# Truer times, a port rule and split output tasks in the list scheduler of a linear-attention and token-mixing kernel

## The chip, the cores and the metric

The kernel runs on one core of a Trainium2 chip. The metric is the time of one execution on the device, in microseconds (us), lower is better. A run counts as slow when it is over 1.5% above the fastest of its kernel.

Engines are named as in the profile: PE does matmuls, DVE is the vector engine, ACT the scalar engine, POOL the GpSimd engine, and SP issues the loads and stores. An instruction line of a profile reads: start, duration, engine, source line, operation, output <- inputs, shape, and in square brackets how long the engine sat idle before it and what ended that wait.

## The reference, cut to what matters

```python
# batch 4, 8 heads, 768 tokens, head size 48
for t in range(S):                       # linear attention with decay
    y[t]  = r[t] @ (state + (u * k[t]) v[t]^T)
    state = w * state + k[t] v[t]^T
x = y as (4, 768, 384)
theta = x @ w_theta
zr, zi = x * cos(theta), x * sin(theta)
y = w_tok_r @ zr + w_tok_i @ zi          # mixing over the 768 tokens
u = x + y
out = u + relu(u @ w_ch)
```

The kernel does the recurrence in chunks of 128 tokens. For a pair of chunks it scales r and k by powers of w (`Rw`, `Kw`), transposes both ("flips"), takes scores, masks them (`mAT`), updates the state (`outer`, `Y`, `Z`, `Sb`), adds the diagonal term (`PD`, `diag`, `dg`, `yd`) and gets `x`. Then come theta, `zr` and `zi`. When a batch is through, its `mix` and `chan` matmuls can run while the next batch is in its first part.

## The kernel before

The program is not written in the order in which it runs. Each piece is a task with an engine, an estimated time and a priority. A list scheduler goes through a simulated time and puts the tasks of each engine in an order; that order is then emitted and is fixed. The engines follow it strictly, each waiting at every task for its inputs (in the trace of before, shown below, PE stands idle for 1.94 us at one such task). So a wrong estimate doesn't change what is computed, only the order.

```python
    def order(self):
        ...
            for e in waiting:
                while free_at[e] <= now:
                    nfree = sum(1 for b in banks if b[0] <= now)
                    best = None
                    for t in waiting[e]:
                        if t.ready <= now and (not t.acq or len(t.acq) + t.keep <= nfree):
                            if best is None or (t.prio, t.seq) < (best.prio, best.seq):
                                best = t
                    ...
                    ns = t.ns
                    if e == PE:
                        if t.mode != last_mode:
                            ns += 100.0
                        last_mode = t.mode
                    free_at[e] = now + ns
...
    def dve_ns(n, rate=1.0):
        return n / (0.96 * rate) + 75
    def pool_ns(n):
        return 190 + 1.95 * n
...
            P.add(PE, 345, scores, rd=[kT, rT], acq=tk, prio=pb + 2, mode=1)
...
            def products(PD=PD, KT=KT, RT=RT):
                nc.vector.tensor_mul(PD, RT, KT)            # both inputs in SBUF
            P.add(DVE, dve_ns(2 * HP * C, 2.0), products, rd=[kT, rT], wr=[kP], prio=pb + 4)
...
            def outputs(...):        # the carried half (RT by Sb), then the inner half (mAT by vb)
            P.add(PE, 720, outputs, rd=[rT] + mk + [kv_] + [("Sb", ...)], acq=ty, prio=pb + 6, mode=1)
```

Of the kernel before, what the change touches and what calls it, by code (L numbers as in the profile page):

```python
# [29 lines left out]

KEEP = 0
LATENCY = {PE: 200.0, DVE: 150.0, ACT: 175.0, POOL: 160.0, SP: 2200.0}


class Task:
    __slots__ = ("eng", "ns", "fn", "deps", "prio", "seq", "lat", "acq", "uses", "nwait",
                 "users", "ready", "end", "mode", "keep")


class Plan:  # L40
# [8 lines left out]

    def add(self, eng, ns, fn, rd=(), wr=(), prio=0.0, lat=None, acq=(), use=(), mode=0, keep=0):  # L50
        t = Task()
        t.eng, t.ns, t.fn, t.prio, t.mode = eng, ns, fn, prio, mode
        t.keep = keep
        t.lat = LATENCY[eng] if lat is None else lat
        t.seq = len(self.tasks)
        t.acq, t.uses = list(acq), list(acq) + list(use)
        rd, wr = list(rd) + list(use), list(wr) + list(acq)
        deps = set()
        for k in rd:
            if k in self.writer:  # L60
                deps.add(self.writer[k])
        for k in wr:
            if k in self.writer:
                deps.add(self.writer[k])
            deps.update(self.readers.get(k, ()))
        for k in rd:
            self.readers.setdefault(k, set()).add(t)
        for k in wr:
            self.writer[k] = t
            self.readers[k] = set()  # L70
        for b in t.uses:
            self.bank_uses[b] = self.bank_uses.get(b, 0) + 1
        deps.discard(t)
        t.deps = deps
        self.tasks.append(t)
        return t

    def order(self):
# [6 lines left out]
        for t in self.tasks:  # L85
            if t.nwait == 0:
                waiting[t.eng].append(t)
        free_at = {e: 0.0 for e in waiting}
        last_mode = None
        banks = [(0.0, i) for i in range(self.nbanks)]  # L90
# [3 lines left out]
        while len(out) < n:  # L94
            for e in waiting:
                while free_at[e] <= now:
                    nfree = sum(1 for b in banks if b[0] <= now)
                    best = None
                    for t in waiting[e]:
                        if t.ready <= now and (  # L100
                                not t.acq or len(t.acq) + t.keep <= nfree):
                            if best is None or (t.prio, t.seq) < (best.prio, best.seq):
                                best = t
                    if best is None:
                        break
                    t = best
                    waiting[e].remove(t)
                    banks.sort()
                    for b in t.acq:
                        self.bank_of[b] = banks.pop(0)[1]  # L110
                    ns = t.ns
                    if e == PE:
                        if t.mode != last_mode:
                            ns += 100.0
                        last_mode = t.mode
                    free_at[e] = now + ns
                    done = now + ns
                    t.end = done + t.lat
                    out.append(t)
                    for b in t.uses:  # L120
                        left[b] -= 1
                        freed[b] = max(freed.get(b, 0.0), t.end)
                        if left[b] == 0:
                            banks.append((freed[b], self.bank_of[b]))
                    for x in t.users:
                        x.ready = max(x.ready, done if x.eng == e else t.end)
                        x.nwait -= 1
                        if x.nwait == 0:
                            waiting[x.eng].append(x)
# [19 lines left out]
def kernel(  # L149
# [91 lines left out]
    def setup():  # L241
# [24 lines left out]
        def pads(ts):  # L266
            for t in ts:
                nc.gpsimd.memset(t[:, :, :, D:], 0.0)
        P.add(POOL, 900, lambda: make_identity(nc, ident_f), wr=["ident_f"], prio=-98)
        P.add(DVE, 200, lambda: nc.vector.tensor_copy(ident, ident_f), rd=["ident_f"],  # L270
              wr=["ident"], prio=-98)
        P.add(POOL, 600, lambda: pads(Rws), wr=[(("Rw", i), j) for i in range(2) for j in range(2)], prio=-97)
# [78 lines left out]
    def token_weights(prio):  # L351
        for to in range(NCH):
            for src, dst, key in ((moe_w_tok_r, WrT, "WrT"), (moe_w_tok_i, WiT, "WiT")):
                i = load_rows(src[to * C:(to + 1) * C, :].rearrange("p (o c) -> p o c", o=2), 2)
                for sg in range(2):
                    tok = ("W", key, to, sg)

                    def flip(i=i, sg=sg, tok=tok):
                        for j in range(3):
# [3 lines left out]
                                             start=(j == 0), stop=(j == 2))  # L363
                    P.add(PE, 330, flip, rd=L2(i) + ["ident_f"], acq=[tok], prio=prio + to)

# [10 lines left out]
    def flip6(dst, blocks, tok, prio, rd, wr):  # L376
# [3 lines left out]
        def go():  # L380
            for i, s in enumerate(blocks):
                nc.tensor.matmul(bank16(tok)[:, i * C:(i + 1) * C], s, ident,  # L382
                                 is_transpose=True, start=(i == 0), stop=(i == n - 1))
        P.add(PE, 55 * n, go, rd=rd + ["ident"], acq=[tok], prio=prio, mode=0)
        P.add(ACT, act_ns(n * C), lambda: nc.scalar.activation(  # L385
# [4 lines left out]
    def front(b, base):  # L390
# [3 lines left out]
        for pr in range(NP):  # L394
# [5 lines left out]
            for c in range(2):  # L400
# [5 lines left out]
                          Ls[ir][:, c * HD:(c + 1) * HD].rearrange("p (h d) -> p h d", h=H), wpow),  # L406
                      rd=[("L", ir, c), "wpow"], wr=[(kR, c)], prio=pb)
            flip6(RT.rearrange("p a h t -> p (a h) t"),
# [6 lines left out]
            for c in range(2):  # L415
                P.add(DVE, dve_ns(HD), lambda c=c, Kw=Kw, ik=ik: nc.vector.tensor_mul(  # L416
                    Kw[:, c, :, :D],
                    Ls[ik][:, c * HD:(c + 1) * HD].rearrange("p (h d) -> p h d", h=H), wpinv),
                    rd=[("L", ik, c), "wpinv"], wr=[kK], prio=pb)
            flip6(KT.rearrange("p a h t -> p (a h) t"),  # L420
# [7 lines left out]
            for c in range(2):  # L428
# [5 lines left out]
                def scores(c=c, tk=tk, KT=KT, RT=RT):  # L434
                    for hp in range(HP):
                        for hi in range(2):
# [3 lines left out]
                                             start=(hp == 0), stop=(hp == HP - 1))  # L440
                P.add(PE, 345, scores, rd=[kT, rT], acq=tk, prio=pb + 2, mode=1)
                for hi in range(2):
# [5 lines left out]
            def products(PD=PD, KT=KT, RT=RT):  # L448
                nc.vector.tensor_mul(PD, RT, KT)  # L449
            P.add(DVE, dve_ns(2 * HP * C, 2.0), products, rd=[kT, rT], wr=[kP],  # L450
                  prio=pb + 4)
            td = ("dg", b, pr)

            def diag(td=td, PD=PD):
# [6 lines left out]
            P.add(PE, 200, diag, rd=[kP, "uw"], acq=[td], prio=pb + 4, mode=0)  # L461
            P.add(ACT, 70, lambda td=td, dg=dg: nc.scalar.activation(
                dg, bank(td)[:, :2 * H], Act.Copy), use=[td], wr=[kd], prio=pb + 4)
# [7 lines left out]
            def outer(ts=ts, Kw=Kw, vb=vb, cs=cs):  # L471
                for c in cs:
                    for hp in range(HP):
                        for hi in range(2):
# [5 lines left out]
                                stop=(c == cs[-1] and hp == HP - 1), skip_group_check=True)  # L480
            P.add(PE, 200 * len(cs), outer, rd=[kK, kv_], acq=[ts], prio=pb + 2, mode=2)
            for c in cs:
# [20 lines left out]

            def outputs(ty=ty, pr=pr, vb=vb, RT=RT):
                first = [True, True]
                for c in range(2):
                    cc = 2 * pr + c
                    if cc == 0:
                        continue
                    for hp in range(HP):  # L510
                        for hi in range(2):
                            q = slice(hi * Dp, (hi + 1) * Dp)
                            o = (c * HP + hp) * D
                            nc.tensor.matmul(bank(ty[hi])[:, o:o + D],
                                             RT[q, c, hp, :],
                                             Sb[q, cc - 1, hp, :], start=first[hi], stop=False,
                                             skip_group_check=True)
                            first[hi] = False
                for c in range(2):
                    mAT = mATs[(b * NCH + 2 * pr + c) % 6]  # L520
                    for hi in range(2):
                        for hp in range(HP):
                            o = (c * HP + hp) * D
                            nc.tensor.matmul(bank(ty[hi])[:, o:o + D], mAT[:, hi, hp, :],
                                             vb[:, c, 2 * hp + hi, :], start=first[hi],
                                             stop=(c == 1 and hp == HP - 1),
                                             skip_group_check=True)
                            first[hi] = False
            P.add(PE, 720, outputs, rd=[rT] + mk + [kv_] + [
                ("Sb", b % 2, 2 * pr + c - 1) for c in range(2) if 2 * pr + c > 0],  # L530
                acq=ty, prio=pb + 6, mode=1)
            for hi in range(2):
# [11 lines left out]
            for t in range(2):  # L544
# [3 lines left out]
                def theta(th=th, t=t, xT=xT):  # L548
                    for dk in range(ND):
                        nc.tensor.matmul(bank(th)[:, :HD], xT[:, t, dk, :], Wth[:, dk, :],  # L550
                                         start=(dk == 0), stop=(dk == ND - 1))
                P.add(PE, 495, theta, rd=[("xT", g % 2), ("Wth", 0), ("Wth", 2)], acq=[th],
                      prio=pb + 8, mode=0)
# [14 lines left out]
    def mixing(b, base):  # L568
        x, zr, zi = xs[b % 3], zrs[b % 2], zis[b % 2]
        xi, zj = b % 3, b % 2  # L570
        for to in range(NCH):
# [5 lines left out]
            for part in range(NP):  # L577
                def mix(tm=tm, to=to, part=part):
                    for j in range(2):
                        so = 2 * part + j  # L580
                        for i, (WT, z) in enumerate(((WrT, zr), (WiT, zi))):
                            nc.tensor.matmul(bank(tm)[:, :HD], WT[:, so, to * C:(to + 1) * C],  # L582
                                             z[:, so], start=(so == 0 and i == 0),
                                             stop=(so == NCH - 1 and i == 1))
                P.add(PE, 660, mix,
                      rd=[(n, zj, 2 * part + j) for n in ("zr", "zi") for j in range(2)]
# [9 lines left out]
            def chan(tf=tf, uT=uT):  # L596
                for dk in range(ND):
                    nc.tensor.matmul(bank(tf)[:, :HD], uT[:, dk, :], Wch[:, dk, :],
                                     start=(dk == 0), stop=(dk == ND - 1))
            P.add(PE, 495, chan, rd=[("uT", g % 3), ("Wch", 0), ("Wch", 2)], acq=[tf],  # L600
                  prio=pb + 1)
# [51 lines left out]
```

## Time and profile before

| | before |
|---|---|
| time, median of 4 runs | 158.73 us (158.64 to 159.06) |
| span of the profiled run | 157.8 us |
| PE, DVE, ACT, POOL busy | 135.7, 120.9, 93.0, 79.0 us |
| matmuls priced at their pace in the trace | 113.6 us |
| changes of PE mode (full-array matmuls and two kinds of half-array ones) | 72, about 95 ns each, 6.8 us |
| PE lost in 0-20, 20-120, 120 us to the last matmul | 15.2, 17.5, 1.8 us |

Busy time of PE is modelled, so each matmul is priced at the usual distance to the next start when PE has work and a full clock (162 ns for 384 columns, 56 ns for a bf16 flip, 109 ns for a float32 flip, 25 to 29 ns for small ones); mode changes are priced at 95 ns (after a mixing matmul the next start comes at 258 ns instead of 162); what a stretch of time holds beyond that is lost, to waits and to a lower clock.

From the page of the kernel before, the busy times:

```profile
PE 135.7 (86%) x1641; PEld 92.8 (59%) x1641; DVE 120.9 (77%) x221; ACT 93.0 (59%) x175; POOL 79.0 (50%) x94
```

From the same page, the span in 40 slices (about 3.9 us each); a digit is the busy share in tenths, and in the third line the granted clock of PE:

```profile
PE   0347789999999979988958999899999999999971
...
DVE  5449796896657999999998899977999956434441
...
PEclk9999999999999999999995699999999999999999
```

The windows view of before (time, then busy us and instructions of PE, PEld, DVE, ACT and POOL, the clock, the DMA share, GB/s), by stretch:

```profile
60.00:80.00 20.00, 18.64 (x287) 12.65 (x285) 20.00 (x37) 15.96 (x29) 15.37 (x18) 1.00 0.92 193
80.00:100.00 20.00, 17.56 (x223) 11.74 (x224) 18.77 (x31) 12.11 (x26) 15.95 (x15) 0.83 0.82 167
```

Over the whole trace of before, the 7 `Kw` and 2 `PD` with less than 30 ns of a POOL operation beside them take 542 to 560 and 678 to 681 ns; the other 17 and 10 take 541 to 1823 and 682 to 1475. The masks (`mAT`), with one input in PSUM, take 673 to 692 ns, beside POOL or not. PE, in the same moments (timeline of before):

```profile
81.80 0.35 PE L457 MATMUL bank_66<-uw,PD_113 128*128 128x2 bf16 x8 [1.94 <-DVE PD_113 L449]
...
82.46 1.03 PE L382 MATMUL bank_66<-ident,Rw_95 128*128 128x128 bf16 x8
...
84.14 1.01 PE L382 MATMUL bank_61<-ident,Kw_97 128*128 128x128 bf16 x8 [0.65 <-DVE mAT_116 L443]
```

PE's next task in the fixed order was the diagonal one, which needs `PD_113`, so PE stood still for 1.94 us. From 82.4 us its clock was half, for 6.8 us: the eight flips that take 0.61 us elsewhere take 1.0 here.

### The profile page before, as it was taken

The page shows a single profiled execution, that of the slowest core. Times are in us where ns is not written, and L with a number is a line of the kernel's source. Part 1 is how long each engine was busy: PE and PEld are TensorE (multiplying, and loading weights), DVE is VectorE, ACT ScalarE, POOL GpSimd, SP SyncE. Part 2 cuts the span into 40 slices and gives each one's busy share as a digit, 9 for nine tenths or more (in the row PEclk, how much of TensorE's full clock was granted, in tenths as well). Part 3 has the DMA queues.
Part 4 walks back from the last instruction along what each step waited for, and adds up shares of the span by engine and source line. Part 5 has one row for each costly group of instructions (what it writes and reads, how often), then busy time and mean ns, then how long its engine had stood idle before and what let it go on. Part 6 is the DMA issues. An engine that isn't in the chain of part 4 may idle for free.

```text
span 157.8 us, 4220 instructions
## 1 busy us (share of the span) xinstructions
PE 135.7 (86%) x1641; PEld 92.8 (59%) x1641; DVE 120.9 (77%) x221; ACT 93.0 (59%) x175; POOL 79.0 (50%) x94
## 2 busy tenths in 40 slices
PE   0347789999999979988958999899999999999971
PEld 0236565698776656656745667367767665666640
DVE  5449796896657999999998899977999956434441
ACT  3593576886955569785846576938935475212120
POOL 6228653650682479595798478526617544000000
PEclk9999999999999999999995699999999999999999
DMA  3999999899993999797989947593100021121212
GB/s 83 216 220 213 225 226 348 325 407 294 198 205 113 192 228 208 174 198 163 227 160 200 208 97 158 119 208 121 54 0 4 25 75 54 50 100 50 104 50 100
DMA packets 81083, 25.24 MB, mean 160 GB/s; under 512 B 75560, under 2 KB 79528, under 8 KB 81064
## 3 DMA queue, kind: packets, MB, share of 16 engines
q1 hardware_dynamic: 81040, 24.98, 65.1%
q8 instruction: 13, 0.21, 0.5%
q14 instruction: 6, 0.05, 0.1%
q10 hardware_dynamic: 24, 0.00, 0.0%
HBM read 20.25 MB, written 4.72 MB: 158 GB/s over the span
## 4 chain that ended last, share of the span: by engine, by line
PE 56%; DVE 22%; ACT 7%; issue 6%; DMA 5%; SPq 1%; POOL 0%; ACTq 0%; DVEq 0%; POOLq 0%
PE bank_64 L582 7%; PE bank_66 L582 5%; PE bank_62 L582 5%; PE bank_65 L582 4%; DMA ld_90<-in_v_dram 3%; DMA ld_86<-in_r_dram 3%; DVE Kw_98 L416 3%; DVE PD_113 L449 2%; DVE mAT_115 L443 2%; PE bank_63 L582 2%; DVE zr_136 L560 2%; PE bank_67 L382 2%; DVE mAT_116 L443 2%; PE bank_61 L382 2%; DVE Kw_97 L416 1%
## 5 line engine op out<-in xcount | busy, mean ns | idle before, releaser
L582 PEld LDWEIGHTS <-WrT 128*128 128x128 bf16 x144 | 14.3, 99 | 7.6 <-issue 0.3
L582 PEld LDWEIGHTS <-WiT 128*128 128x128 bf16 x144 | 14.3, 99 | 7.3 <-issue 0.3
L494 POOL TENSOR_TENSOR Z_122<-Y_120,wC 128x192 f32<-128x192 f32 x12 | 6.1, 507 | 12.8 <-DVE Y_120 L491 6.5
L563 POOL TENSOR_TENSOR zi_137<-x_132,sin_139 128x384 bf16<-128x384 bf16 x4 | 3.7, 943 | 9.9 <-ACT sin_139 L554 9.9
L494 POOL TENSOR_TENSOR Z_123<-Y_121,wC 128x192 f32<-128x192 f32 x8 | 5.3, 663 | 5.3 <-DVE Y_121 L491 5.3
L404 POOL TENSOR_TENSOR Rw_96<-ld_85,wpow 128x384 bf16<-128x384 f32 x6 | 6.2, 1048 | 3.5 <-PE bank_68 L382 3.5
L582 PE MATMUL bank_64<-zr_135,WrT 128*128 128x384 bf16 x18 | 5.9, 327 | 0.0
L582 PE MATMUL bank_64<-zi_137,WiT 128*128 128x384 bf16 x18 | 5.9, 326 | 0.0
L582 PE MATMUL bank_62<-zr_136,WrT 128*128 128x384 bf16 x18 | 5.9, 326 | 0.0
L582 PE MATMUL bank_62<-zi_138,WiT 128*128 128x384 bf16 x18 | 5.9, 326 | 0.0
L582 PE MATMUL bank_64<-zr_136,WrT 128*128 128x384 bf16 x18 | 5.9, 326 | 0.0
L582 PE MATMUL bank_64<-zi_138,WiT 128*128 128x384 bf16 x18 | 5.9, 326 | 0.0
L582 PE MATMUL bank_66<-zi_137,WiT 128*128 128x384 bf16 x18 | 5.9, 326 | 0.0
L582 PE MATMUL bank_66<-zr_135,WrT 128*128 128x384 bf16 x18 | 5.8, 325 | 0.0
L550 PEld LDWEIGHTS <-xT_141 128*128 128x128 bf16 x36 | 3.7, 107 | 3.3 <-issue 1.4
L404 POOL TENSOR_TENSOR Rw_95<-ld_88,wpow 128x384 bf16<-128x384 f32 x4 | 5.0, 1276 | 0.6 <-PE bank_67 L382 0.6
L449 DVE TENSOR_TENSOR PD_112<-RT_106,KT_110 128x1024 bf16<-128x1024 bf16 x3 | 3.3, 1092 | 2.6 <-ACT KT_110 L385 2.6
L404 POOL TENSOR_TENSOR Rw_96<-ld_91,wpow 128x384 bf16<-128x384 f32 x4 | 3.9, 997 | 2.2 <-DMA ld_91<-in_r_dram 2.2
L283 PE MATMUL bank_61<-ident_f,wu 8*128 8x8 f32 x1 | 0.2, 240 | 5.6 <-DMA wu<-in_u_dram 5.6
L563 POOL TENSOR_TENSOR zi_138<-x_132,sin_140 128x384 bf16<-128x384 bf16 x4 | 3.6, 910 | 2.6 <-ACT sin_140 L554 2.6
L563 POOL TENSOR_TENSOR zi_137<-x_134,sin_139 128x384 bf16<-128x384 bf16 x4 | 3.6, 910 | 2.4 <-ACT sin_139 L554 2.4
L550 PEld LDWEIGHTS <-xT_142 128*128 128x128 bf16 x36 | 3.4, 97 | 2.3 <-ACT xT_142 L385 0.2
(602 smaller groups left out, 521.5 us busy)
## 6 DMA issues: line engine op xcount, KB each, us to landing
out_dram<-fin_149 SPq DMA_DIRECT2D x8, 192.0 KB, 1.8
out_dram<-fin_150 SPq DMA_DIRECT2D x8, 192.0 KB, 1.9
out_dram<-fin_151 SPq DMA_DIRECT2D x8, 192.0 KB, 1.8
ld_85<-in_r_dram SPq DMA_DIRECT2D x6, 192.0 KB, 5.3
ld_86<-in_k_dram SPq DMA_DIRECT2D x6, 192.0 KB, 4.0
ld_87<-in_v_dram SPq DMA_DIRECT2D x6, 192.0 KB, 3.8
ld_88<-in_r_dram SPq DMA_DIRECT2D x4, 192.0 KB, 3.5
ld_89<-in_k_dram SPq DMA_DIRECT2D x4, 192.0 KB, 3.5
```

Of the source, the lines that this page charges most:

```text
L283: nc.tensor.matmul(bank("wu")[:, :2 * HP], wu.rearrange("p a d -> p (a d)"), ident_f[:2 * HP, :2 * HP], is_transpose=True, start=True, sto ...
L382: nc.tensor.matmul(bank16(tok)[:, i * C:(i + 1) * C], s, ident, is_transpose=True, start=(i == 0), stop=(i == n - 1))
L404: lambda c=c, vec=vec, Rw=Rw, ir=ir: vec.tensor_mul(Rw[:, c, :, :D], Ls[ir][:, c * HD:(c + 1) * HD].rearrange("p (h d) -> p h d", h=H), wpow),
L416: P.add(DVE, dve_ns(HD), lambda c=c, Kw=Kw, ik=ik: nc.vector.tensor_mul(Kw[:, c, :, :D], Ls[ik][:, c * HD:(c + 1) * HD].rearrange("p (h d) ...
L443: P.add(DVE, dve_ns(HP * C), lambda hi=hi, tk=tk, mAT=mAT: nc.vector.tensor_mul(mAT[:, hi], bank(tk[hi]).rearrange("p (h t) -> p h t", h=H ...
L449: nc.vector.tensor_mul(PD, RT, KT)
L494: P.add(POOL, pool_ns(HP * D) - 70, lambda cc=cc: nc.gpsimd.tensor_mul(Zs[cc % 2], Ys[cc % 2], wide(wC, D)), rd=[("Y", cc % 2), "wC"], wr= ...
L550: nc.tensor.matmul(bank(th)[:, :HD], xT[:, t, dk, :], Wth[:, dk, :], start=(dk == 0), stop=(dk == ND - 1))
L560: P.add(DVE, dve_ns(HD), lambda th=th, to=to: nc.vector.tensor_mul(zr[:, to], bank(th)[:, :HD], x[:, to]), use=[th], rd=xk, wr=[("zr", zj, ...
L563: P.add(POOL, pool_ns(HD), lambda sn=sn, to=to, t=t: nc.gpsimd.tensor_mul(zi[:, to], x[:, to], sn[:, t]), rd=xk + [("sin", g % 2, t)], wr= ...
L582: nc.tensor.matmul(bank(tm)[:, :HD], WT[:, so, to * C:(to + 1) * C], z[:, so], start=(so == 0 and i == 0), stop=(so == NCH - 1 and i == 1))
```

## The change

The intent is a plan that is nearer to the machine: PE times read from a trace, mode changes counted, DVE instructions with two SBUF inputs (`Kw`, `PD` and one `Rw`) never planned beside a POOL operation (the "port rule", after the program's name `port` for the mark on such tasks), and output matmuls in two tasks so that the half that needs no masks can go first. The diff, cut to its core:

```diff
+SWITCH = 95.0
+STAY = 10.0
...
+        held = {DVE: 0.0, POOL: 0.0}
...
                     for t in waiting[e]:
+                        if t.port and e in (DVE, POOL) and held[POOL if e == DVE else DVE] > now:
+                            continue
...
-                            if best is None or (t.prio, t.seq) < (best.prio, best.seq):
-                                best = t
+                            rank = (t.prio - (STAY if e == PE and t.mode == last_mode and last_mode else 0.0), t.seq)
+                            if best is None or rank < top:
+                                best, top = t, rank
...
-                            ns += 100.0
+                            ns += SWITCH
...
+                    if t.port:
+                        held[e] = now + ns
...                                          # port=True: Kw, PD, the one Rw on DVE, all of POOL
-        P.add(POOL, 900, lambda: make_identity(nc, ident_f), ...)
-        P.add(DVE, 200, lambda: nc.vector.tensor_copy(ident, ident_f), ...)
+        P.add(POOL, 500, lambda: make_identity(nc, ident_f), ...)
+        P.add(POOL, 500, lambda: make_identity(nc, ident), ...)
...
-                P.add(PE, 345, scores, ...)
+                P.add(PE, 230, scores, ...)
-            P.add(PE, 200 * len(cs), outer, ...)
+            P.add(PE, 125 * len(cs), outer, ...)
...                                          # smaller: 330 to 328, 55n to 56n, 495 to 487, 660 to 649; ACT dg 70 to 140
-            P.add(PE, 720, outputs, rd=[rT] + mk + [kv_] + [("Sb", ...)], acq=ty, prio=pb + 6, mode=1)
+            P.add(PE, 100 * len(cq), carried, rd=[rT] + [("Sb", ...)], acq=ty, prio=pb + 6, mode=1)
+            P.add(PE, 400, inner, rd=mk + [kv_], use=ty, wr=ty, prio=pb + 6)
```

The inner task also goes half by half (`for hi: for c:`) where the old one went chunk by chunk (`for c: for hi:`).

More of the change, by code (lines that the diff above doesn't have):

```diff
@@ L36 @@
     __slots__ = ("eng", "ns", "fn", "deps", "prio", "seq", "lat", "acq", "uses", "nwait",
-                 "users", "ready", "end", "mode", "keep")
+                 "users", "ready", "end", "mode", "keep", "port")
 class Plan:
@@ L48, in __init__, with add @@
         self.bank_of = {}
-    def add(self, eng, ns, fn, rd=(), wr=(), prio=0.0, lat=None, acq=(), use=(), mode=0, keep=0):
+    def add(self, eng, ns, fn, rd=(), wr=(), prio=0.0, lat=None, acq=(), use=(), mode=0, keep=0, port=False):
         t = Task()
         t.eng, t.ns, t.fn, t.prio, t.mode = eng, ns, fn, prio, mode
-        t.keep = keep
+        t.keep, t.port = keep, port or eng == POOL
         t.lat = LATENCY[eng] if lat is None else lat
@@ L268, in pads @@
                 nc.gpsimd.memset(t[:, :, :, D:], 0.0)
-        P.add(POOL, 900, lambda: make_identity(nc, ident_f), wr=["ident_f"], prio=-98)
-        P.add(DVE, 200, lambda: nc.vector.tensor_copy(ident, ident_f), rd=["ident_f"],
-              wr=["ident"], prio=-98)
+        P.add(POOL, 500, lambda: make_identity(nc, ident_f), wr=["ident_f"], prio=-98)
+        P.add(POOL, 500, lambda: make_identity(nc, ident), wr=["ident"], prio=-98)
         P.add(POOL, 600, lambda: pads(Rws), wr=[(("Rw", i), j) for i in range(2) for j in range(2)], prio=-97)
@@ L363, in flip @@
                                              start=(j == 0), stop=(j == 2))
-                    P.add(PE, 330, flip, rd=L2(i) + ["ident_f"], acq=[tok], prio=prio + to)
+                    P.add(PE, 328, flip, rd=L2(i) + ["ident_f"], acq=[tok], prio=prio + to)
                     def evac(sg=sg, tok=tok, dst=dst, to=to):
@@ L383, in go @@
                                  is_transpose=True, start=(i == 0), stop=(i == n - 1))
-        P.add(PE, 55 * n, go, rd=rd + ["ident"], acq=[tok], prio=prio, mode=0)
+        P.add(PE, 56 * n, go, rd=rd + ["ident"], acq=[tok], prio=prio, mode=0)
         P.add(ACT, act_ns(n * C), lambda: nc.scalar.activation(
@@ L406, in front @@
                           Ls[ir][:, c * HD:(c + 1) * HD].rearrange("p (h d) -> p h d", h=H), wpow),
-                      rd=[("L", ir, c), "wpow"], wr=[(kR, c)], prio=pb)
+                      rd=[("L", ir, c), "wpow"], wr=[(kR, c)], prio=pb, port=True)
             flip6(RT.rearrange("p a h t -> p (a h) t"),
@@ L418, in front @@
                     Ls[ik][:, c * HD:(c + 1) * HD].rearrange("p (h d) -> p h d", h=H), wpinv),
-                    rd=[("L", ik, c), "wpinv"], wr=[kK], prio=pb)
+                    rd=[("L", ik, c), "wpinv"], wr=[kK], prio=pb, port=True)
             flip6(KT.rearrange("p a h t -> p (a h) t"),
@@ L440, in scores @@
                                              start=(hp == 0), stop=(hp == HP - 1))
-                P.add(PE, 345, scores, rd=[kT, rT], acq=tk, prio=pb + 2, mode=1)
+                P.add(PE, 230, scores, rd=[kT, rT], acq=tk, prio=pb + 2, mode=1)
                 for hi in range(2):
@@ L450, in front @@
             P.add(DVE, dve_ns(2 * HP * C, 2.0), products, rd=[kT, rT], wr=[kP],
-                  prio=pb + 4)
+                  prio=pb + 4, port=True)
             td = ("dg", b, pr)
@@ L461, in front @@
             P.add(PE, 200, diag, rd=[kP, "uw"], acq=[td], prio=pb + 4, mode=0)
-            P.add(ACT, 70, lambda td=td, dg=dg: nc.scalar.activation(
+            P.add(ACT, 140, lambda td=td, dg=dg: nc.scalar.activation(
                 dg, bank(td)[:, :2 * H], Act.Copy), use=[td], wr=[kd], prio=pb + 4)
@@ L480, in outer @@
                                 stop=(c == cs[-1] and hp == HP - 1), skip_group_check=True)
-            P.add(PE, 200 * len(cs), outer, rd=[kK, kv_], acq=[ts], prio=pb + 2, mode=2)
+            P.add(PE, 125 * len(cs), outer, rd=[kK, kv_], acq=[ts], prio=pb + 2, mode=2)
             for c in cs:
@@ L502, in front, with carried @@
             mk = [("mAT", (b * NCH + 2 * pr + c) % 6, hi) for c in range(2) for hi in range(2)]
-            def outputs(ty=ty, pr=pr, vb=vb, RT=RT):
-                first = [True, True]
-                for c in range(2):
-                    cc = 2 * pr + c
-                    if cc == 0:
-                        continue
+            cq = [c for c in range(2) if 2 * pr + c > 0]
+            def carried(ty=ty, pr=pr, RT=RT, cq=cq):
+                for c in cq:
                     for hp in range(HP):
@@ L513, in outputs, with inner @@
                             o = (c * HP + hp) * D
-                            nc.tensor.matmul(bank(ty[hi])[:, o:o + D],
-                                             RT[q, c, hp, :],
-                                             Sb[q, cc - 1, hp, :], start=first[hi], stop=False,
+                            nc.tensor.matmul(bank(ty[hi])[:, o:o + D], RT[q, c, hp, :],
+                                             Sb[q, 2 * pr + c - 1, hp, :],
+                                             start=(c == cq[0] and hp == 0), stop=False,
                                              skip_group_check=True)
-                            first[hi] = False
-                for c in range(2):
-                    mAT = mATs[(b * NCH + 2 * pr + c) % 6]
-                    for hi in range(2):
+            P.add(PE, 100 * len(cq), carried,
+                  rd=[rT] + [("Sb", b % 2, 2 * pr + c - 1) for c in cq],
+                  acq=ty, prio=pb + 6, mode=1)
+            def inner(ty=ty, pr=pr, vb=vb):
+                for hi in range(2):
+                    for c in range(2):
+                        mAT = mATs[(b * NCH + 2 * pr + c) % 6]
                         for hp in range(HP):
@@ L524, in outputs @@
                             nc.tensor.matmul(bank(ty[hi])[:, o:o + D], mAT[:, hi, hp, :],
-                                             vb[:, c, 2 * hp + hi, :], start=first[hi],
+                                             vb[:, c, 2 * hp + hi, :], start=False,
                                              stop=(c == 1 and hp == HP - 1),
                                              skip_group_check=True)
-                            first[hi] = False
-            P.add(PE, 720, outputs, rd=[rT] + mk + [kv_] + [
-                ("Sb", b % 2, 2 * pr + c - 1) for c in range(2) if 2 * pr + c > 0],
-                acq=ty, prio=pb + 6, mode=1)
+            P.add(PE, 400, inner, rd=mk + [kv_], use=ty, wr=ty, prio=pb + 6)
             for hi in range(2):
@@ L551, in theta @@
                                          start=(dk == 0), stop=(dk == ND - 1))
-                P.add(PE, 495, theta, rd=[("xT", g % 2), ("Wth", 0), ("Wth", 2)], acq=[th],
+                P.add(PE, 487, theta, rd=[("xT", g % 2), ("Wth", 0), ("Wth", 2)], acq=[th],
                       prio=pb + 8, mode=0)
@@ L584, in mix @@
                                              stop=(so == NCH - 1 and i == 1))
-                P.add(PE, 660, mix,
+                P.add(PE, 649, mix,
                       rd=[(n, zj, 2 * part + j) for n in ("zr", "zi") for j in range(2)]
@@ L599, in chan @@
                                      start=(dk == 0), stop=(dk == ND - 1))
-            P.add(PE, 495, chan, rd=[("uT", g % 3), ("Wch", 0), ("Wch", 2)], acq=[tf],
+            P.add(PE, 487, chan, rd=[("uT", g % 3), ("Wch", 0), ("Wch", 2)], acq=[tf],
                   prio=pb + 1)
```

## The prediction

-2, -1, +0.8, -0.7 and -0.5 come to -3.4, put as "about -3.5", so 155.3 us.

> **What bounds it now.** The page's first part gives PE 135.7 us busy of 158, DVE 120.9, ACT 93.0, POOL 79.0; the chain of waits is PE 56%, DVE 22%, ACT 7%. Busy PE time is modelled, so I priced matmuls by their start-to-start pace in the trace: mixing, theta and channel 162 ns, bf16 flips 56, float32 flips 109, and so on: 113.6 us. A change between full-array and half-array matmuls costs about 95 ns (258 ns after a mixing matmul, not 162); before has 72 of them, 6.8 us. The rest, about 37 us, is PE lost: 15 us in the first 20, 5 in 20-30, about 12 in 50-120, 4.7 at the end. Of the 12, about 3.4 is one stretch of 6.8 us at half the granted clock (slice view, 82-89 us). After 120 us PE has no holes. So only what shrinks holes before 120 us counts.
>
> **What makes the holes.** DVE is busy 20.0 of 20 us in 60-80 us (windows view). Its multiplies with both inputs in SBUF stretch: Kw takes 541 ns alone, up to 1823 (excess of 24: 7.8 us), PD 678, up to 1475 (3.1 us). Mask multiplies, one input in PSUM, stay at 673-692. [...] About 11 of 121 us of DVE are this.
>
> **What the change does.** Nearly the same instructions in another order.
> 1. Port: the plan keeps Kw, PD and the DVE Rw off POOL's operations. But the order is static and its DVE times stay too short (475 ns for 541, 608 for 675), so overlaps return by drift. I expect the excess to fall from 11 to about 6 us, of which about 2 us shows as fewer PE holes.
> 2. PE times nearer to the trace (scores 345 to 230): mixing matmuls ahead of the last scores rise from 152 to 184 of 288 (built order). About 1 us of holes.
> 3. Mode switches: the built order has 80, not 72: +0.8 us. [...]
> 4. Splitting carried from inner output matmuls: little.
> 5. Opening: the DVE cast of ident goes, and wup is copied before Rw, so ACT's second table load (1.28 us, at 7.77) begins about 1 us sooner; RT_106 at 9.07 waits on it. About -0.7 us.
>
> Sum: -2 -1 +0.8 -0.7, and -0.5 from the 20-30 us stretch: about -3.5 us, 155.3 us. Range 152.5 to 159.0. Chances: faster by over 2% (under 155.6) 0.53, within 2% 0.43, slower 0.04.
>
> **What would show it.** Kw's mean falls from 867 ns to about 680, PD's from 930 to about 800, DVE busy to about 115; masks unchanged. RT_106 starts near 8.3 us. Holes in 50-120 us shrink by about 3 us. The half-clock stretch stays one, of about 7 us.
>
> **What would make it wrong.** Better: port avoidance holds in execution (Kw near 560 ns), DVE frees 10 us, about 152 us. Worse: a second half-clock stretch (+3.4 us); static DVE orders that wait on PE (x before Kw's second half in the second pair), holding up flips behind them; or the loads (DMA share 0.8-1.06 to 100 us) becoming the limit.

## More of the kernel before

DVE is full in the middle. And PE's clock drops in the slices at 82 to 89 us.

The timeline of before around that place, DVE first, then POOL:

```profile
78.28 0.79 DVE L449 TENSOR_TENSOR PD_112<-RT_108,KT_110 128x1024 bf16<-128x1024 bf16 x1
78.99 1.35 DVE L416 TENSOR_TENSOR Kw_97<-ld_89,wpinv 128x384 bf16<-128x384 f32 x1
80.26 1.48 DVE L449 TENSOR_TENSOR PD_113<-RT_109,KT_111 128x1024 bf16<-128x1024 bf16 x1
81.66 1.82 DVE L416 TENSOR_TENSOR Kw_97<-ld_89,wpinv 128x384 bf16<-128x384 f32 x1
...
78.48 2.71 POOL L404 TENSOR_TENSOR Rw_95<-ld_88,wpow 128x384 bf16<-128x384 f32 x2
81.15 1.92 POOL L464 TENSOR_TENSOR yd_129<-dg_126,vb_102 128x768 bf16<-128x768 f32 x1
```

`Kw` takes 541 ns at its shortest and `PD` 678, so these four DVE instructions, 5.4 us together, should have taken 2.4. POOL was busy beside all of them.

## The result, and the profile after

The changed kernel takes 150.2 us (median of 4 runs, 149.75 to 150.49) against 158.73 us. The ratio is 0.9457, 95% interval 0.9429 to 0.9485. A ratio here is the mean time of one kernel's fast runs over the mean of the other's in the same rounds, so it is not quite the ratio of the medians quoted beside it. The time lies below the stated range of 152.5 to 159.0: the prediction had the direction right and the size wrong, 3.5 us forecast and 8.5 measured.

The page after, busy times and slices (about 3.7 us each):

```profile
PE 131.8 (89%) x1641; PEld 91.7 (62%) x1641; DVE 114.0 (77%) x220; ACT 92.4 (62%) x175; POOL 79.4 (53%) x96
...
PE   0268669999999999999979999999999999999970
...
DVE  0249699799757979969999999999799956652531
...
PEclk9999999999999999999999999999999999999997
```

The clock no longer drops before the end, where PE has finished (half from 146.95 us, the last matmul ends at 145.25). The windows view after:

```profile
60.00:80.00 20.00, 18.99 (x249) 12.73 (x247) 18.25 (x34) 14.79 (x27) 14.61 (x16) 1.00 1.04 219
80.00:100.00 20.00, 19.91 (x287) 13.70 (x286) 19.35 (x38) 13.97 (x28) 15.68 (x16) 1.00 0.89 193
```

In 80-100 us PE now does 287 matmuls where it did 223 (over 60-100 us, 536 where it did 510). DVE is about as full as before, and PE waits less. The one larger wait left in 30-120 us is of the same kind as before, and shows how the port rule fails in places. POOL, DVE and PE in the timeline after:

```profile
74.16 1.47 POOL L471 TENSOR_TENSOR yd_129<-dg_126,vb_102 128x768 bf16<-128x768 f32 x1 [0.68 <-ACT dg_126 L469]
...
74.20 2.31 DVE L423 TENSOR_TENSOR Kw_100<-ld_86,wpinv 128x384 bf16<-128x384 f32 x2
...
77.55 0.61 PE L389 MATMUL bank_68<-ident,Kw_100 128*128 128x128 bf16 x8 [0.85 <-DVE zr_136 L566]
```

POOL began 40 ns before DVE, and the two `Kw` instructions took 2.31 us. The flips of `Kw_100` waited for their bank, which DVE's `zr_136` frees, and `zr_136` stood behind the stretched `Kw`: PE lost about 0.9 us. PE lost in each stretch:

| stretch, us | lost before | lost after |
|---|---|---|
| 0-20 | 15.2 | 15.2 |
| 20-30 | 4.9 | 4.1 |
| 30-60 | 2.3 | 0.7 |
| 60-80 | 2.3 | 2.1 |
| 80-100 | 5.6 | 0.5 |
| 100-120 | 2.3 | 1.0 |
| 120 to the last matmul | 1.8 | 1.4 |

The sum falls by 9.4 us; eight more mode changes (80 for 72) give 0.8 back.

### The profile page after: what moved, and what is told of

The parts are those of the page before. It is cut to its first block, busy times and chain, and to the rows that moved or that the text cites. A ratio compares the mean times of both kernels' runs of the same rounds, so it can differ in the third digit from the quotient of the medians.

```text
span 148.8 us, 4211 instructions
## 1 busy us (share of the span) xinstructions
PE 131.8 (89%) x1641; PEld 91.7 (62%) x1641; DVE 114.0 (77%) x220; ACT 92.4 (62%) x175; POOL 79.4 (53%) x96
## 4 chain that ended last, share of the span: by engine, by line
PE 64%; DVE 12%; DMA 9%; ACT 8%; issue 3%; POOL 1%; SPq 0%; ACTq 0%
PE bank_65 L588 8%; PE bank_63 L588 6%; PE bank_61 L588 4%; PE bank_67 L588 4%; DMA ld_87<-in_v_dram 3%; DMA ld_90<-in_v_dram 3%; DMA wu<-in_u_dram 2%; PE bank_68 L604 2%; DVE mAT_114 L450 2%; PE bank_67 L556 2%; PE bank_61 L389 2%; PE bank_68 L389 1%; PE bank_66 L389 1%; PE bank_64 L389 1%; DVE Kw_100 L423 1%
## 5 line engine op out<-in xcount | busy, mean ns | idle before, releaser
L501 POOL TENSOR_TENSOR Z_122<-Y_120,wC 128x192 f32<-128x192 f32 x12 | 7.9, 657 | 6.2 <-DVE Y_120 L498 3.2
L501 POOL TENSOR_TENSOR Z_123<-Y_121,wC 128x192 f32<-128x192 f32 x8 | 5.0, 621 | 3.5 <-DVE Y_121 L498 3.4
L569 POOL TENSOR_TENSOR zi_137<-x_132,sin_139 128x384 bf16<-128x384 bf16 x4 | 3.8, 967 | 4.4 <-ACT sin_139 L560 4.3
L588 PE MATMUL bank_67<-zr_135,WrT 128*128 128x384 bf16 x18 | 5.9, 329 | 0.0
L569 POOL TENSOR_TENSOR zi_138<-x_132,sin_140 128x384 bf16<-128x384 bf16 x4 | 3.7, 947 | 4.1 <-ACT sin_140 L560 4.1
L588 PE MATMUL bank_65<-zr_135,WrT 128*128 128x384 bf16 x18 | 5.9, 327 | 0.0
L588 PE MATMUL bank_61<-zr_136,WrT 128*128 128x384 bf16 x18 | 5.9, 327 | 0.0
L588 PE MATMUL bank_65<-zr_136,WrT 128*128 128x384 bf16 x18 | 5.9, 327 | 0.0
L588 PE MATMUL bank_63<-zr_136,WrT 128*128 128x384 bf16 x18 | 5.9, 326 | 0.0
L588 PE MATMUL bank_67<-zi_137,WiT 128*128 128x384 bf16 x18 | 5.9, 326 | 0.0
L588 PE MATMUL bank_65<-zi_137,WiT 128*128 128x384 bf16 x18 | 5.9, 326 | 0.0
L588 PE MATMUL bank_61<-zi_138,WiT 128*128 128x384 bf16 x18 | 5.9, 326 | 0.0
L588 PE MATMUL bank_65<-zi_138,WiT 128*128 128x384 bf16 x18 | 5.9, 326 | 0.0
L588 PE MATMUL bank_63<-zi_138,WiT 128*128 128x384 bf16 x18 | 5.9, 326 | 0.0
L588 PE MATMUL bank_63<-zr_135,WrT 128*128 128x384 bf16 x18 | 5.9, 326 | 0.0
L588 PE MATMUL bank_63<-zi_137,WiT 128*128 128x384 bf16 x18 | 5.9, 326 | 0.0
```

Source lines behind the costliest of these rows:

```text
L501: P.add(POOL, pool_ns(HP * D) - 70, lambda cc=cc: nc.gpsimd.tensor_mul(Zs[cc % 2], Ys[cc % 2], wide(wC, D)), rd=[("Y", cc % 2), "wC"], wr= ...
L569: P.add(POOL, pool_ns(HD), lambda sn=sn, to=to, t=t: nc.gpsimd.tensor_mul(zi[:, to], x[:, to], sn[:, t]), rd=xk + [("sin", g % 2, t)], wr= ...
L588: nc.tensor.matmul(bank(tm)[:, :HD], WT[:, so, to * C:(to + 1) * C], z[:, so], start=(so == 0 and i == 0), stop=(so == NCH - 1 and i == 1))
```

## The experiments

Eighteen kernels were run, all correct, each timed in three rounds against the kernel before on its own chip. All are edits of one of the two kernels. Two theories stood at the start. Theory A: the hole at 80 us, made by the port, also halves PE's clock, and the port rule is the main part. The rivals: the clock drops by itself (B), the truer PE times do it (C). More came later. The table gives the results, the text after it the reasoning. Times are medians of four runs; what is read from a trace comes from one of the four (for `a_dve135` the slow one, whose three fast runs have a median of 154.6 us).

| kernel | edit | us | ratio to before | PE lost in 20-120 us | mean Kw, PD, ns | DVE busy, us |
|---|---|---|---|---|---|---|
| before | | 158.7 | 1 | 17.5 | 867, 937 | 120.9 |
| b_sw | before, other draw | 158.8 | 0.995 (0.989-1.001) | 16.6 | 799, 1027 | 120.3 |
| b_fill | before, hole filled | 156.9 | 0.985 (0.980-0.991) | 15.5, 1.6 of it filler | 841, 919 | 119.9 |
| b_times | before + PE times | 155.8 | 0.978 (0.972-0.984) | 13.3 | 805, 832 | 117.4 |
| b_port | before + port rule | 153.4 | 0.964 (0.958-0.969) | 12.1 | 803, 860 | 118.5 |
| b_port_times | before + both | 153.3 | 0.963 (0.960-0.967) | 11.1 | 790, 891 | 118.6 |
| after | | 150.2 | 0.946 (0.943-0.949) | 8.3 | 777, 711 | 114.0 |
| a_sw | after, other draw | 150.6 | 0.946 (0.942-0.950) | 8.5 | 702, 784 | 113.9 |
| a_nostay | after, STAY off | 150.1 | 0.942 (0.936-0.948) | 8.2 | 725, 782 | 113.7 |
| a_unsplit | after, one output task | 152.8 | 0.959 (0.954-0.965) | 10.7 | 760, 859 | 116.0 |
| a_unsplit_sw | same, other draw | 151.9 | 0.952 (0.945-0.958) | 9.7 | 768, 734 | 114.7 |
| a_cmajor | after, inner by chunk | 152.4 | 0.956 (0.948-0.964) | 9.4 | 760, 709 | 114.3 |
| a_noport | after, no port rule | 156.5 | 0.983 (0.976-0.990) | 13.6 | 804, 872 | 116.1 |
| a_noport_sw | same, other draw | 154.8 | 0.969 (0.963-0.975) | 12.7 | 813, 935 | 117.2 |
| a_oldtimes | after, old PE times | 156.0 | 0.977 (0.971-0.984) | 14.8 | 817, 732 | 116.4 |
| a_old_sw | same, other draw | 153.7 | 0.963 (0.956-0.970) | 12.2 | 702, 861 | 114.5 |
| a_dve135 | after, DVE times + 60 ns | 155.2 | 0.970 (0.961-0.979) | 13.0 | 620, 728 | 111.8 |
| a_warm2 | after, warmed PE | 154.3 | 0.967 (0.958-0.976) | 11.6 | 778, 685 | 114.1 |
| a_true | after, all times at pace | 151.7 | 0.951 (0.945-0.957) | 10.1 | 732, 789 | 114.3 |
| a_true_sw | same, other draw | 150.3 | 0.944 (0.936-0.952) | 8.1 | 627, 749 | 111.6 |

Over the twenty profiled runs, the span rises by 1.02 us for each us of PE lost in 20-120 us (correlation 0.987). That is nearly bookkeeping, since the matmuls are the same and the two ends hardly change. But it says where all differences sit. DVE busy follows the span much less (0.74): `a_dve135` has one of the two lowest DVE times, and its span is among the five longest (in its slow run).

### The hole and the clock: b_fill

Ten matmuls that nobody uses go into the free bank of the one diagonal task that waited in before. The plan and all other orders are unchanged.

```diff
             def diag(td=td, PD=PD, pr=pr):
+                if (b, pr) == (2, 1):
+                    for j in range(10):
+                        nc.tensor.matmul(bank(td)[:, :HD], WrT[:, 0, :C], Wth[:, 0, :],
+                                         start=True, stop=True, skip_group_check=True)
```

> The kernel before with ten filler matmuls (WrT by Wth, 384 columns) into the free diagonal bank ahead of the one diagonal task that waited 1.94 us for PD at 80 us; the order of everything else is untouched. Theory A (a hole in PE, made by the port stall, triggers the half-clock stretch at 82-89 us): the stretch goes, the clock reads about 0.99 or more, and about 3 us go with it (155.5 to 156 us), although DVE's stall stays as long. Rival B (the stretch comes at its own time, not by idleness): the stretch stays and the time is 158.7 or a little more.

Measured: 156.9 us, ratio 0.985. The granted clock was 0.995 to 0.999 in its four runs, and 0.975 to 0.986 in the seven of before beside it. The page of `b_fill` (clock by slice), and the fillers, the diagonal matmuls and the next flips in its timeline:

```profile
PEclk9999999999999999999999999999999999999999
```

```profile
79.82 1.80 PE L458 MATMUL bank<-Wth,WrT 128*128 128x384 bf16 x10
81.88 0.35 PE L462 MATMUL bank<-uw,PD 128*128 128x2 bf16 x8 [0.26 <-DVE PD L450]
...
82.53 0.62 PE L383 MATMUL bank<-ident,Rw 128*128 128x128 bf16 x8
```

DVE's stall is as long as before (the diagonal task starts at 81.88 us, in before at 81.80), but with PE kept busy the clock stays up, the flips take 0.62 us where they took 1.03, and about 2.2 us are gone. Theory A stands here and B falls: the half-clock stretch is an effect of the hole. It is less than the 3 us I expected.

### One part at a time: b_port, b_times, a_noport, b_port_times

`b_port` adds only the port rule to before, `b_times` only the PE times (with the ACT time of `dg`), `b_port_times` both, and `a_noport` takes the port rule out of the changed kernel.

```diff
 a_noport:
-                        if t.port and e in (DVE, POOL) and held[POOL if e == DVE else DVE] > now:
+                        if False:
```

> The kernel before with the port rule alone added (flags on Kw, PD, DVE Rw and all of POOL), old PE times, no other part. Theory A: most of the gain, 151 to 154 us, no half-clock stretch before the end, PD near 700 ns. Rival C: 157 to 159 us.

> The kernel before with the PE times of the change alone (scores 230, outer 125 a chunk, outputs 600, switch 95), no port rule. Theory A: little, 156 to 159 us, Kw and PD as stretched as before. Rival C: most of the gain, 151 to 154 us.

> The changed kernel with the port rule of the plan switched off, everything else kept. Theory A (the port rule is the main part): Kw and PD stretch again (Kw's mean back to about 860 ns, PD's to about 930), PE holes of 3 us or more return in 50-120 us, time 154 to 159 us. Rival C (the truer PE times and the preference for the same mode are the main part): 150 to 152 us.

> The kernel before with both main parts, the port rule and the truer PE times, but with no preference for the same mode, the outputs in one task and ident cast on DVE. If these two parts make the change (theory A, mended: each alone gave 153.4 and 155.8), 150 to 151.5 us. If the split outputs or the mode preference matter (rival D), 152.5 us or more.

Measured: 153.4, 155.8, 156.5 and 153.3 us. None of the four shows a half clock before its last matmul. Against `b_fill`, which has the old order without the clock loss, the port rule alone is worth 3.5 us more and the PE times alone 1.1. Together they are worth no more than the port rule alone. So neither theory fits whole: the port rule is the largest part in these single draws, but port rule and times lack 3 us of the change. Nor is it shown that the rule gained in `b_port` by sparing DVE: I had expected `PD` near 700 ns there and it stayed at 860, and `b_times`, without the rule, has `Kw` and `PD` as short (805 and 832 for 803 and 860). In the changed kernel they are 777 and 711.

### The split and the mode: a_unsplit, a_nostay, a_cmajor

`a_unsplit` puts the output matmuls back into one task of 600 ns. `a_nostay` sets STAY to 0. `a_cmajor` keeps two tasks and only puts the inner one back to chunk by chunk.

```diff
 a_cmajor:
-                for hi in range(2):
-                    for c in range(2):
+                for c in range(2):
+                    for hi in range(2):
```

> The changed kernel with the output matmuls put back into one task of 600 ns. Theory A: within 1 us of the changed kernel, 149.5 to 151.5 us. Rival D (the split lets PE begin earlier and that matters): 152 us or more, with more PE lost in 30-120 us.

> The changed kernel with the preference for the mode that PE is in switched off (the switch cost stays counted). Theory A: within 1 us of the changed kernel. Rival D (keeping the mode matters): more than 80 mode changes in the trace and 1 us or more longer.

> The changed kernel, its second output task going chunk by chunk as before instead of half by half; everything else and the order of tasks the same. If the split gains because the first bank of outputs ends half a task sooner (rival E), 151.5 us or more. If it gains because the carried half no longer waits for the masks (theory A): within 0.7 us of the changed kernel.

Measured: 152.8, 150.1 and 152.4 us. The preference for the same mode does nothing measurable: 80 mode changes with it and without. The split is worth about 2 us in this draw, which I had called little. `a_cmajor` points to how. It keeps the order of the tasks, so no luck of the order (next section) enters, and its 152.4 us falls where I had put rival E: most of what the split gained goes when the first bank of outputs ends later. It is not settled: the runs spread from 151.5 to 153.0, the ratio of 0.956 (0.948 to 0.964) just overlaps that of the changed kernel, and PE lost in 20-120 us is 9.4 for 8.3 in the profiled run, the fastest of the four.

### Luck of the order: a_sw, b_sw, a_old_sw, a_noport_sw, a_unsplit_sw, and a_oldtimes

A list scheduler jumps: a small change of a number can reorder everything behind it. Five controls repeat a kernel with the switch cost in the plan moved by 10 ns. They tell how much any two kernels may differ for no reason.

```diff
-SWITCH = 95.0
+SWITCH = 105.0
```

> A control: the changed kernel with the switch cost in the plan at 105 instead of 95 ns. Nothing of meaning changes, only the order that the plan falls into. It tells how much of a difference between two of these kernels is luck of the order: I expect 149.5 to 151.5 us; if it is off by over 1.5 us, differences of that size between the other kernels prove nothing.

> A control: the kernel before with the switch cost in the plan at 110 instead of 100 ns; only the order it falls into differs. If before is a fair sample of its plan: 158 to 160 us. If part of the gain is that before fell into an unlucky order (one hole that halves the clock): about 156 to 157 us, with no half-clock stretch before the end.

> A control: the kernel a_oldtimes (the changed one with the old PE times, 156.0 us) with the switch cost at 105 instead of 95 ns. If its loss of nearly 6 us is due to the old PE times: 154.5 to 157.5 us. If it was luck of the order: under 153 us.

> A control: the kernel a_noport (the changed one without the port rule, 156.5 us) with the switch cost at 105 instead of 95 ns. If the loss is due to the missing port rule: 155 to 158 us. If it was luck of the order: under 153.5 us.

> A control: the kernel a_unsplit (the changed one with the outputs in one task, 152.8 us) with the switch cost at 105 instead of 95 ns. If the split is worth 2 us or more by itself: 152 to 154 us. If it was luck of the order: 150 to 151.3 us.

`a_oldtimes` keeps port rule and split but puts the old PE times back.

> The changed kernel with the old PE times in the plan (scores 345, outer 200 a chunk, flips 55, the two output tasks 140 a chunk and 440), port rule and split kept. Theory A, mended again (the port rule and the split make the change, the truer PE times add nothing once the port rule is there): 150 to 151.3 us. Rival C (the PE times matter with the split): 152.5 us or more.

Measured: the two draws of before differ by 0.1 us in their medians, of the changed kernel by 0.4, unsplit by 1.0, without the port rule by 1.7, with the old times by 2.2. Four of these are not what I had written down: `b_sw` has no half-clock stretch and is still no faster (its holes lie elsewhere, 4.3 us lost in 80-100 us), and `a_noport_sw`, `a_old_sw` and `a_unsplit_sw` fell between my two branches. So a difference of 1 to 2 us between two single kernels proves nothing here. What holds in both draws: taking out the port rule costs 4.6 and 6.3 us, the old PE times 3.5 and 5.8, the single output task 1.7 and 2.6 (medians, against 150.2). These sum to more than the gain. Port rule and PE times cost more than the 2.2 us that luck made here, so each is needed for the whole; the split's 1.7 and 2.6 do not clear it by themselves. No part has a price of its own.

### The plan's DVE times: a_dve135, a_true, a_true_sw

My prediction called the plan's DVE times too short, 475 ns for 541 and 608 for 675. `a_dve135` lengthens them by 60 ns. (With 66 ns, the exact difference, the plan got stuck; that kernel did not build.)

```diff
-        return n / (0.96 * rate) + 75
+        return n / (0.96 * rate) + 135
```

> The changed kernel with the DVE times of the plan raised by 60 ns each, to what the trace shows (535 for 541, 668 for 675). If drift of the plan's DVE times is what leaves Kw stretched (mean 777 ns, up to 1842), Kw and PD fall under 650 and 720 ns and the time by 1 us or more, to 148 to 149.5 us. If not, 150 us or above.

Measured: 155.2 us, or 154.6 without its slow run, 4.4 us longer. The trace is of the slow run (156.4 us). `Kw` did stretch less (mean 620 ns) and DVE was busy for only 111.8 us. PE's waits in 60-100 us of `a_dve135` (who waited for whom: us in total, times, longest) are no longer on `PD` or `Kw`:

```profile
PE bank L464 <- ACT dg L469: 1.4, 1, 1.4
PE bank L588 <- ACT RT L392: 1.1, 1, 1.1
```

Behind both stand loads: ACT's `dg` was queued behind a `vb` that waited for a load, and ACT's `RT` needed flips of an `Rw` that waited for one (waits of ACT and POOL in the same stretch):

```profile
ACT vb L431 <- DMA ld<-in_v_dram: 3.6, 1, 3.6
POOL Rw L411 <- DMA ld<-in_r_dram: 4.3, 1, 4.3
```

In this slow run the clock also dropped once, for 3.4 us at 79 us, after start-to-start holes of 1.54 and 1.33 us. Its mean clock is 0.988; the three fast runs have 0.994 to 1.000, so they give no sign of such a drop. What I had missed shows in two DVE lines of the kernel before:

```profile
13.61 0.68 DVE L443 TENSOR_TENSOR mAT_115<-bank_66,mask_71 128x512 bf16<-128x512 f32 x1
14.21 0.68 DVE L443 TENSOR_TENSOR mAT_115<-bank_67,mask_71 128x512 bf16<-128x512 f32 x1
```

Each lasts 0.68 us, but the second starts 0.60 us after the first: the records overlap. Start to start, a mask takes 598 ns and a 384-column instruction 465 ns (medians over the trace after). The plan's 608 and 475 were right, and the "correction" made them false. So `a_dve135`, like `a_oldtimes`, gives one engine false times, and it loses too (4.4 us, in one draw, against 3.5 and 5.8). That the false times cost it that much is not shown: in its one trace PE hangs on late loads, and it has no second draw.

If false times lose, do truer ones gain? `a_true` sets DVE, ACT and POOL to their pace in the trace; the largest error was POOL's `yd`, 1688 ns in the plan and 1432 in the trace.

```diff
-        return n / (0.96 * rate) + 75
+        return n / (0.96 * rate) + 65
-        return 190 + 1.95 * n
+        return {384: 868, 768: 1432, 192: 535}[n]      # Rw has 955
```

> The changed kernel with the plan's DVE, ACT and POOL times set to the start-to-start pace in its trace (DVE 465 and 598 ns instead of 475 and 608, ACT 10 ns less, POOL 868, 1432 and 465 instead of 939, 1688 and 494, Rw 955). Theory F (how true the plan's times are decides how many holes PE gets; the DVE times were true already, which is why raising them by 60 ns cost 5 us): 147 to 150 us and under 8.4 us of PE lost in 20-120 us. Rival G (the rest is luck of the order): 150 to 153 us.

> A second draw of the same: a_true with the switch cost at 105 instead of 95 ns. Theory F: 147 to 150 us as well. Rival G: anything from 149.5 to 153 us, and over 1 us from a_true.

Measured: 151.7 and 150.3 us. Theory F falls: neither kernel is under 150 us, and `a_true` has 10.1 us of PE lost. Neither is faster than the changed kernel by more than the luck of the order. `a_true_sw` has Kw at a mean of 627 ns and 8.1 us of PE lost: a still better port record bought nothing. No version beat the changed kernel clearly.

### The cold start of PE: a_warm2

In both kernels the matmuls go at half pace until about 27 us: bf16 flips start 107 ns apart, later 56. (The slice view prints a 9 there: the trace has no record of the clock before 27.8 us in before and 27.5 after, so the pace has to be read from the matmuls.) `a_warm2` fills PE's early empty time with 30 matmuls on a memset tile.

```diff
         def wu_flip():
+            for j in range(14):
+                nc.tensor.matmul(bank("wu")[:, :HD], warm[:, :C], warm[:, :HD], start=True, ...)
...                                  # 5 and 3 ahead of two score tasks, 7 ahead of a flip, 1 ahead of a carried task
```

> The changed kernel with filler matmuls (a memset tile, 384 columns) in PE's empty time of the first 16 us: 14 ahead of the first transposition, 5 and 3 ahead of two score tasks, 7 and 1 elsewhere. In the changed kernel the matmuls up to 27 us go at half pace (flips 107 ns apart, later 56). If activity lifts the half clock, [...] flips before 27 us fall to 56 ns, and 1 to 3 us go: 147.5 to 149.5 us. If it falls back between, or the opening hangs on loads and DVE alone: 149.7 to 151 us.

Measured: the clock was full from 10.9 us, but fell back at 27.9 us for 3.4 us, and the time is 154.3 us. The profiled run has a mean clock of 0.986; the other three have 0.952 to 0.958, so they lost more to the clock than the trace shows. Nothing came sooner: the second pair's scores start at 19.1 us (19.2 in the changed kernel), the first mixing matmul at 41.0 (39.5). The longest wait of PE in 18-30 us of `a_warm2` says why:

```profile
PE bank L374 <- DMA ld<-in_moe_w_tok_r_dram: 1.5, 1, 1.5
```

In this run the opening hangs on loads and on what they release, not on PE's pace. Why the whole is 4 us slower is shown only in part.

## Why the prediction was right or wrong

**Right: PE's holes before 120 us are the whole matter.** The last stretch is as full in both kernels, and all twenty runs line up with PE lost in 20-120 us.

**Right: the size of the DVE excess.** I expected the stretching of `Kw` and `PD` to fall from 11 to about 6 us. It fell from 10.9 to 6.0 (5.6 for `Kw`, 0.4 for `PD`); DVE busy went from 120.9 to 114.0, forecast about 115. The split between the two was wrong: `Kw` came to 777 ns (forecast 680), `PD` to 711 (forecast 800). One place where it fell and one where the longest grew, minimum, median and maximum in ns, `PD` and `Kw` of before, then of after:

```profile
L449 DVE TENSOR_TENSOR PD_113<-RT_109,KT_111 x3: 681/1052/1475, 49.7 to 120.8; 128x1024 bf16<-128x1024 bf16 x3
...
L416 DVE TENSOR_TENSOR Kw_100<-ld_86,wpinv x6: 542/554/893, 44.9 to 105.9; 128x384 bf16<-128x384 f32 x6
```

```profile
L456 DVE TENSOR_TENSOR PD_113<-RT_109,KT_111 x3: 678/692/794, 46.4 to 112.9; 128x1024 bf16<-128x1024 bf16 x3
...
L423 DVE TENSOR_TENSOR Kw_100<-ld_86,wpinv x6: 546/548/1842, 42.1 to 101.6; 128x384 bf16<-128x384 f32 x6
```

The masks kept their 673 to 693 ns. What goes with the stretching is POOL: over the traces of before and after, the 16 `Kw` and 4 `PD` with less than 30 ns of a POOL operation beside them took 542 to 560 and 677 to 681 ns, the other 32 and 20 took 541 to 1842 and 678 to 1475, and the 81 masks beside POOL 673 to 692. Not all that ran beside POOL stretched, and by what mechanism the others did is not shown.

**Wrong: "The half-clock stretch stays one, of about 7 us".** This is one term that failed. I counted 3.4 us of lost clock and took it as given. It was an effect of the 1.94 us hole; `b_fill` shows it, and prices it at 2.2 us. That the port stall made the hole is read from the timeline (5.4 us of DVE for 2.4). The order of the two stood in the trace of before, so the question was there to be asked: PE's wait ends at 81.80 us, and the clock is half from 82.36 to 89.19. The length of a single hole alone doesn't decide it. Holes of 1.46 us in `b_sw` and of 1.77 in `a_noport_sw` (start to start; the one in before is 2.16 so) had no drop behind them; in `a_dve135` (slow run) a drop of 3.4 us followed holes of 1.54 and 1.33. What separates the cases is not shown.

**Wrong: "of which about 2 us shows as fewer PE holes".** This is the other term, of about the same size. I took a share of DVE's saved time. But, as the timelines read, a hole is not made by DVE's load. It is made where the fixed order puts a PE task ahead of its input, and it ends when that one input comes (in before, the 1.94 us ended with `PD_113`). With the clock left out, PE lost in 20-120 us fell by about 6 us (9.2 less the 3.4, half of 6.8, that I put down to the clock; by `b_fill`'s price of 2.2, 7) where I had 3.5 for port, times and the 20-30 us stretch together. `a_true_sw` shows the two apart: `Kw` at 627 ns for 777, and PE lost 8.1 us for 8.3.

**Wrong: "its DVE times stay too short ... so overlaps return by drift".** The durations of records are not the pace. At their pace the plan's DVE times were right, and the kernel with longer ones was 4.4 us slower (in one draw). Overlaps do return (`Kw_100` at 74.2 us), but not for that reason.

**Wrong: "Splitting carried from inner output matmuls: little".** It is 1.7 to 2.6 us in two draws, about as much as luck alone made elsewhere. **Undersized: PE times, "about 1 us".** With port rule and split in place, the old times cost 3.5 to 5.8 us. I priced the parts one by one and added; the parts work together.

**Right, but worth nothing: the opening.** `RT_106` started at 8.39 us, forecast 8.3. ACT in before, then after:

```profile
7.77 1.28 ACT L308 ACT_TABLE_LOAD   x1
9.07 1.02 ACT L385 ACTIVATE RT_106<-bank_62 128x1024 bf16<-128x1024 bf16 x1
```

```profile
7.10 1.28 ACT L315 ACT_TABLE_LOAD   x1
8.39 1.02 ACT L392 ACTIVATE RT_106<-bank_62 128x1024 bf16<-128x1024 bf16 x1
```

But the second pair's scores start at 19.2 us, in before at 18.7, and PE lost in the first 20 us is 15.2 in both: the 0.7 us that I had forecast did not come. The risk that I had named came true: `x` now stands ahead of the second half of `Kw_98` on DVE, and that half starts at 16.03 us and takes 1.38.

**Right: mode changes.** 80 instead of 72 in the trace, as built, at about 95 ns each (258 ns to the next start after a mixing matmul instead of 162). "PE mode switches counted" describes the plan; it did not lower their number.

**Open.** How the split gains its 2 us (an earlier start of the carried half, or an earlier end of the first bank, which `a_cmajor` favours) is not settled. By which holes the port rule gains is not shown either: in `b_port` the stretching hardly differs from `b_times`. What the loads cost was not tested, although the DMA share is 0.82 to 1.04 in 60-100 us. How the 8.5 us divide among port rule, times and split has no answer that holds from draw to draw, beyond the ranges above.

## What to carry to other kernels

Where engines follow fixed orders, a task placed ahead of its input costs its whole wait (1.94 us of PE at one task of before), so the times in a plan should be true in pace (start to start), not in recorded duration: old PE times lost 3.5 and 5.8 us here, though making the other engines' times truer as well gained nothing. A drop of the granted clock can be a consequence (here 6.8 us at half clock behind that wait, gone in `b_fill`): look at what PE waited for just before it, and fill that hole once to see what the clock alone is worth. Before a single part of a scheduler change is given a price, draw the order again with a constant moved a little; here that alone was up to 2.2 us.
